# The fourth group's second layer by seven products in six of eight pairs

## The chip, the cores and the metric

The kernel runs on one core of one Trainium2 chip. The metric is the device time of one execution in microseconds (us), as the median of several runs. The engines are called by their names in the profile: PE (TensorE; PEld is its weight load), DVE (VectorE), ACT (ScalarE), POOL (GpSimd) and SP (SyncE, which issues most transfers).

## The reference

The input is 4 batches of 8 heads with 768 positions of 64 values. Each position attends to the first 8 positions and to the last 96 up to itself, with a bias that falls with the distance. The result, 3072 tokens of 512 values, goes through a two-layer network:

```python
h = x @ w_in                                                  # 512 -> 2048
g = np.where(h > 0.0, h, alpha * (np.exp(np.minimum(h, 0.0)) - 1.0))
return (g @ w_out).astype(np.float32)                         # 2048 -> 512
```

## The kernel before

**Groups and slices.** The tokens go in 12 groups of 256 (two tiles of 128). The 2048 hidden values go in 16 slices of 128. For a slice and a group, the first layer (`up`) makes a 128x256 block `h` in one PSUM bank, ACT and DVE make the activation `g` of it, and the second layer (`down`) adds the slice's product with its 128x512 weights to the output banks. Every factor is kept as a rounded part and a remainder (HI and LO; `gh` and `gl`), so that each product is three terms: `up` is 12 matmuls of 256 columns, and a plain `down` (line 880, in `moe`) is two tiles by three terms, 6 matmuls of 512 columns.

**Order of the groups.** The weights arrive in the first quarter. Groups one to three go through the slices together, four slices at a time, with partial outputs kept in the tiles `pa0` to `pa5`. Then the fourth group (index `NE` = 3; about 203 to 256 us) goes plainly through all 16 slices (`moe`), and groups five to twelve (index `SE` = 4 and on) go through `seven`. The attention of the next group runs beside: four visits per group, in which PE makes the scores of one pair of heads and the weighted values of an earlier one (lines 474 and 610), DVE, ACT and POOL make the softmax (lines 462, 464, 482, 580), and the probabilities are turned by a store to DRAM and a load back (lines 589 and 596).

**Seven products.** `seven` takes slices in pairs `j`. The activations of a pair are four blocks (two slices by two tiles), the weights four blocks (two slices by left and right half of 256 columns). The eight block products are replaced by seven: `combine` makes four sums of activation blocks on DVE (lines 733 to 736; tile `sum7`), rounds raw blocks and sums on ACT (`rh`, `sh`; line 303) and makes their remainders on DVE (`rl`, `sl`; line 311). `down` then multiplies them (line 768): products 1, 2, 4 first, then 6 and 5, then 3 and 7, each three matmuls of 256 columns, 21 in all. Products 2, 3 and 4 (as `mix` tiles) and 5 (in the right half of `w0`) need sums of weight blocks. The products stay apart in four banks `o0` to `o3` until the group's end, where one copy on ACT and seven adds on DVE (line 798) make the two output tiles.

**The weight sums.** `prepare`, one call per pair, adds up the whole weights (`hl`, line 672), makes four differences (`tf`), rounds each (`mix`, lines 303 and 305, ACT or POOL) and takes the remainder (line 311, DVE or POOL), and stores it to DRAM (line 668). This runs beside the end of group three and group four, in the order of `j`, in tiles `pa0` to `pa5`. `swap` then stores the old right half of each `w0` (line 695; needed for a rarely taken branch at the end) and loads the first sum in its place (line 696), after group four. Sums two to four are loaded again for each pair and group (line 751): three loads of 256 KB.

**Who sets the order.** The order of all work is written out ahead. Each piece of work (`p.add`) has a due time, engines it can run on with modelled costs, and the tiles it reads and writes; a list scheduler (`Plan.order`) takes on each engine what can start first and among these what is due first. `early` holds a piece back until a time. A tile class takes its places in the order of its pieces (`SLOTS`); each engine then runs its list strictly in that order, SP too, whose list holds all transfers and their waits. In groups one to four, `h` has four banks (`WIDE`: `h0`, `h1`, `v0`, `t0`); `seven` has two (`h0`, `h1`), since `v0` and `t0` are its banks `o2` and `o3`.

## Time and profile before

| | |
|---|---|
| median of 3 runs | 644.73 us (644.15 to 644.75) |
| the profiled execution | 644.23 us, of which the span of its instructions is 642.4 us |
| PE busy | 631.0 us, 98% of the span |
| PEld busy | 584.4 us, 91% |
| DVE busy | 492.7 us, 77% |
| ACT, POOL busy | 411.0 and 199.1 us |
| granted PE clock, mean | 0.997 |
| DMA | 149.82 MB, mean 233 GB/s |

Times in the trace run from the span's start. Matmuls are pipelined, so an engine that is 98% busy need not be at its peak; the distance from one start to the next says what an instruction takes of PE. An instruction that reads `x4` stands for four in a row. A landing time runs from the issue of a transfer to its semaphore.

### The profile page before, as it was taken

Reading aid. Unit: us, or ns where it says so; the run is one execution under the profiler, and the core shown is the slowest. Engines: PE = TensorE matmul, PEld = TensorE weight load, DVE = VectorE, ACT = ScalarE, POOL = GpSimd, SP = SyncE. Lnnn points to the kernel's source line nnn. Section 1 sums busy time; section 2 is a strip of 40 time slices with the busy share of each in tenths; the row PEclk is TensorE's granted clock in tenths of the full one; section 3 lists DMA queues with packets and bytes.
Section 4 is the critical chain, followed back from the end, with each engine's and each line's share of the span. In section 5 each row is a group of like instructions: output and inputs, shape, how many; then the busy total and the mean of one; then the engine's idle time right before and its main releaser. Section 6 shows DMA issues by size and latency. Waiting matters only on the chain.

```text
span 642.4 us, 19164 instructions
## 1 busy us (share of the span) xinstructions
PE 631.0 (98%) x7054; PEld 584.4 (91%) x7054; DVE 492.7 (77%) x1648; ACT 411.0 (64%) x1201; POOL 199.1 (31%) x500
## 2 busy tenths in 40 slices
PE   8999999999999999999999999999999999999996
PEld 5878888898888889999999999999999999999996
DVE  6999888899878975777777777777686777776654
ACT  6999776666644665666666566576566566654553
POOL 3557465465467672121121121112022022020000
PEclk9999999999999999999999999999999999999998
DMA  8979934231365899788888888888888788875542
GB/s 309 376 283 408 342 84 125 70 108 62 87 220 211 260 300 295 250 269 246 270 252 282 258 251 264 277 259 253 273 253 243 254 283 260 277 233 165 181 149 86
DMA packets 131171, 149.82 MB, mean 233 GB/s; under 512 B 63616, under 2 KB 82816, under 8 KB 131072
## 3 DMA queue, kind: packets, MB, share of 16 engines
q1 hardware_dynamic: 130784, 148.41, 71.7%
q8 instruction: 57, 0.93, 0.6%
q14 instruction: 42, 0.34, 0.2%
q10 hardware_dynamic: 288, 0.13, 0.1%
HBM read 117.57 MB, written 30.93 MB: 231 GB/s over the span
## 4 chain that ended last, share of the span: by engine, by line
PE 89%; DVE 4%; ACT 3%; DMA 2%; issue 1%; POOL 0%; DVEq 0%; POOLq 0%; ACTq 0%
PE h L712 28%; PE o L768 24%; PE o L880 13%; PE h L854 12%; PE s L610 5%; PE s L474 4%; PE pv L507 2%; DMA qk<-in_qkv_dram 1%; ACT pr L464 1%; PE t L527 1%; DMA n_raw<-in_n_dram 1%; DVE pr L462 1%; DMA mixed<-mix 1%; PE t L529 0%; DVE g L395 0%
## 5 line engine op out<-in xcount | busy, mean ns | idle before, releaser
L712 PE MATMUL h<-xh,w 128*128 128x256 f32 x1024 | 142.2, 280 | 0.8 <-DVE gg L722 0.8
L712 PEld LDWEIGHTS h<-xh,w 128*128 128x128 f32 x1024 | 129.8, 188 | 3.0 <-issue 1.2
L722 DVE SCALAR_TENSOR_TENSOR gg<-e,h 128x256 f32<-128x256 f32 x128 | 53.4, 417 | 76.0 <-ACT e L721 74.9
L580 POOL TENSOR_SCALAR pr<-pr,st 128x168 f32<-128x168 f32 x144 | 62.6, 435 | 152.1 <-DVE st L482 139.3
L464 ACT ACTIVATE pr<-pr,nmax 128x168 f32<-128x168 f32 x192 | 81.8, 427 | 16.9 <-DVE nmax L462 16.3
L720 ACT ACTIVATE e<-h 128x256 f32<-128x256 f32 x128 | 48.7, 381 | 58.4 <-PE h L712 58.4
L854 PEld LDWEIGHTS h<-xh,w 128*128 128x128 f32 x512 | 76.9, 188 | 9.9 <-DVE h L862 0.2
L880 PE MATMUL o<-w,gh 128*128 128x512 f32 x256 | 81.6, 400 | 0.4 <-DVE ob L912 0.4
L712 PE MATMUL h<-xl,w 128*128 128x256 f32 x512 | 81.8, 281 | 0.0
L854 PE MATMUL h<-xh,w 128*128 128x256 f32 x512 | 81.5, 282 | 0.0
L712 PEld LDWEIGHTS h<-xl,w 128*128 128x128 f32 x512 | 69.4, 188 | 2.0 <-issue 1.7
L462 DVE CUSTOM_DVE_ANT_0 pr<-s,far 128x168 f32<-128x168 f32 x192 | 53.3, 325 | 11.8 <-ACT xh L303 11.1
L311 POOL TENSOR_TENSOR w<-g,w 128x256 fp32r<-128x256 f32 x64 | 50.8, 816 | 35.7 <-ACT w L303 29.8
L303 ACT CAST sh<-sum 128x512 fp32r<-128x512 f32 x64 | 39.8, 621 | 30.9 <-DVE sum L736 30.9
L585 DVE STREAM_TRANSPOSE tr<-pr 128x192 f32<-128x192 f32 x144 | 50.0, 364 | 11.2 <-POOL pr L580 10.7
L721 ACT ACTIVATE e<-e 128x256 f32<-128x256 f32 x128 | 53.4, 417 | 3.6
L768 PE MATMUL o<-mix,sh 128*128 128x256 f32 x256 | 51.1, 281 | 0.0
L880 PEld LDWEIGHTS o<-w,gh 128*128 128x128 f32 x256 | 43.0, 188 | 7.9 <-ACT e L860 1.0
L451 POOL TENSOR_SCALAR qk<-qk,scale 128x256 f32<-128x256 f32 x14 | 8.0, 570 | 135.6 <-DMA qk<-in_qkv_dram 68.1
L311 DVE TENSOR_TENSOR sl<-sum,sh 128x512 fp32r<-128x512 f32 x64 | 44.2, 691 | 5.7 <-ACT sh L303 5.7
L768 PE MATMUL o<-w,sh 128*128 128x256 f32 x256 | 48.1, 280 | 0.0
L303 ACT CAST rh<-gg 128x384 fp32r<-128x384 f32 x64 | 32.8, 513 | 20.1 <-DVE gg L722 19.5
(142 smaller groups left out, 1418.9 us busy)
## 6 DMA issues: line engine op xcount, KB each, us to landing
mix<-mixed SPq DMA_DIRECT2D x192, 256.0 KB, 4.6
qk<-in_qkv_dram SPq DMA_DIRECT2D x48, 312.0 KB, 4.1
v<-in_qkv_dram SPq DMA_DIRECT2D x36, 384.0 KB, 5.0
dd<-tr SPq DMA_DIRECT2D x36, 384.0 KB, 4.6
pt<-dd SPq DMA_DIRECT2D x72, 192.0 KB, 3.8
bits<-in_w_in_dram SPq DMA_DIRECT2D x16, 512.0 KB, 8.5
bits<-in_w_out_dram SPq DMA_DIRECT2D x16, 512.0 KB, 9.7
mixed<-mix SPq DMA_DIRECT2D x32, 256.0 KB, 3.2
```

The source lines that it names most:

```text
L303: self.nc.scalar.copy(out, x)
L311: self.on(e).tensor_tensor(out, x, y, ALU.subtract)
L462: first = p.add((("DVE", 85 + 1.042 * LW, False),), lambda e: nc.vector.tensor_tensor_reduce(x(), s.t[:, i, :LW], tab, -(2.0 ** -(h + 1)), ...
L464: p.add(act(LW, extra=200), lambda e: nc.scalar.activation(x(), x(), AF.Exp, bias=nm, scale=-1.0, accum_out=st.t[:, n, 0:1]), [pr], [pr, s ...
L580: nc.gpsimd.tensor_scalar(pr.t[:, :LW], pr.t[:, :LW], st.t[:, n, 3:4], 1.0, ALU.mult, ALU.mult)
L585: nc.vector.transpose(tr.t[:, :, i, j], pr.t.rearrange("p (b r) -> p b r", r=32))
L712: nc.tensor.matmul(h.t, w1.t[:, s, cc * P:(cc + 1) * P], self.chunk(x, cc), start=n == 0 and s == HI and cc == 0, stop=n == 1 and cc == se ...
L721: p.add(act(W), lambda e: nc.scalar.activation(ex.t, ex.t, AF.Exp, scale=-1.0), [ex], [ex], d - 8000)
L722: p.add(dve(W), lambda e: nc.vector.scalar_tensor_tensor(gs(), ex.t, -1.0, h.t, ALU.add, ALU.max), [h, ex], [g], d - 8000)
L768: nc.tensor.matmul(acc[bank].t[:, half], a, b.t[:, LO if t == 1 else HI, x], start=j == 0 and t == 0 and n in first, stop=j == self.NFC // ...
L854: nc.tensor.matmul(h.t, w1.t[:, s, cc * P:(cc + 1) * P], self.chunk(x, cc), start=n == 0 and cc == 0, stop=n == 2 and cc == self.NCC - 1)
L880: nc.tensor.matmul(o.t[:, :at.stop - at.start], g.t[:, i * P:(i + 1) * P], w2.t[:, s, at], start=fc == f0 and n == 0 and s == HI, stop=fc ...
```

## The change

The fourth group goes through `seven` as well. Its first two pairs (`DIRECT` = 2) are multiplied plainly there, in `direct`: the eight block products, three terms each, as 24 matmuls of 256 columns, with the eighth output half in the free half of bank `o3`. Pairs three to eight go by seven products. `prepare` takes these six pairs first and the two plain ones last; the plain ones' pieces come after the fourth group's in the list. The first sum is written by ACT or POOL and DVE or POOL into the right half of `w0` itself, so its store and its reload are gone; the old half is stored before (`keep`), not earlier than a set time (138 us in the planner's clock for the first pair, 9 us more for each further one). Stored sums now use the class `mixed` with the two places `pa0` and `pa1`; the fourth group's loads use `pa2` to `pa5`, its `sum7` the places `io0` and `io1`. Its group end has one more add, for the eighth half. Its `h` has two banks, not four.

```diff
@@ -661,9 +661,11 @@
             return dve(n) + pool(n)
 
         def stored(n, tf, d):
-            x = self.sb("mix", "mix", [P, 2, M], F32R)
-            p.add(act(M) + pool(M, False), lambda e: self.copy(e, x.t[:, HI], tf.t), [tf], [x], d)
-            p.add(two(M), lambda e: self.minus(e, x.t[:, LO], tf.t, x.t[:, HI]), [tf, x], [x], d + 10)
+            x, at, after = (w0, right, [self.kept[j]]) if n == 1 else (self.sb("mixed", "mix", [P, 2, M], F32R), left, [])
+            p.add(act(M) + pool(M, False), lambda e: self.copy(e, x.t[:, HI, at], tf.t), [tf, *after], [x], d)
+            p.add(two(M), lambda e: self.minus(e, x.t[:, LO, at], tf.t, x.t[:, HI, at]), [tf, x], [x], d + 10)
+            if n == 1:
+                return
             s = self.mixed[j][n] = self.dr(f"mix{j}{n}", "mixed", [P, 2, M])
             p.add(sp(), lambda e: nc.sync.dma_start(s.t, x.t.bitcast(F32)), [x], [s], d + 30, nbytes=P * M * 8)
 
@@ -686,20 +688,18 @@
         stored(2, t2, due + 310)
         stored(4, less(r1, left, t2, slice(0, M), due + 400), due + 410)
 
-    def swap(self, j, due):
+    def keep(self, j, due):
 
         nc, p, M = self.nc, self.plan, self.DM // 2
-        w0, x = self.ws[1][2 * j], self.mixed[j][1]
-        right = slice(M, 2 * M)
+        w0 = self.ws[1][2 * j]
         self.kept[j] = kept = self.dr(f"kept{j}", "kept", [P, 2, M])
-        p.add(sp(), lambda e: nc.sync.dma_start(kept.t, w0.t[:, :, right].bitcast(F32)), [w0], [kept], due, nbytes=P * M * 8)
-        p.add(sp(), lambda e: nc.sync.dma_start(w0.t[:, :, right].bitcast(F32), x.t), [x, kept], [w0], due + 10, nbytes=P * M * 8)
-
-    def seven(self, rows, xh, xl, dues, step, last):
+        p.add(sp(), lambda e: nc.sync.dma_start(kept.t, w0.t[:, :, M:].bitcast(F32)), [w0], [kept], due, nbytes=P * M * 8, early=due)
+
+    def seven(self, rows, xh, xl, dues, step, last, plain=None):
 
         nc, p, M = self.nc, self.plan, self.DM // 2
         left, right = slice(0, M), slice(M, 2 * M)
-        acc = {}
+        acc, begun = {}, set()
         G = {}
 
         def up(fc, d):
@@ -723,7 +723,14 @@
 
         def combine(j, d):
             g = G[j]
-            s = self.sb("sum7", "sum7", [P, 4, P])
+            if j < (plain or 0):
+                gh, gl = (self.sb(x, x, [P, 4, P], F32R) for x in ("sh", "sl"))
+                whole = lambda x: x.t.rearrange("p a t -> p (a t)")
+                p.add(act(4 * P), lambda e: self.copy(e, whole(gh), whole(g)), [g], [gh], d - 8000)
+                p.add(dve(4 * P), lambda e: self.minus(e, whole(gl), whole(g), whole(gh)), [g, gh], [gl], d - 7000)
+                G[j] = gh, gl
+                return
+            s = self.sb("sum7", "sum7", [P, 4, P], slots=self.SUMS if plain is not None else None)
             rh, rl = self.sb("rh", "rh", [P, 3, P], F32R), self.sb("rl", "rl", [P, 3, P], F32R)
             sh, sl = (self.sb(x, x, [P, 4, P], F32R) for x in ("sh", "sl"))
             flat = lambda x: x.rearrange("p a t -> p (a t)")
@@ -742,36 +749,66 @@
             p.add(dve(4 * P), lambda e: self.minus(e, flat(sl.t), flat(s.t), flat(sh.t)), [s, sh], [sl], d - 6500)
             G[j] = rh, rl, sh, sl
 
+        def opened():
+            if not acc:
+                for i in range(6 if last else 4):
+                    acc[i] = self.bank(f"o{i}", "o", [P, 2, M])
+
+        def direct(j, d):
+
+            gh, gl = G.pop(j)
+            ws = self.ws[1][2 * j:2 * j + 2]
+            opened()
+            for f, w in enumerate(ws):
+                for c, terms in enumerate(((0, 1), (2,))):
+                    todo = []
+                    for i in range(NT):
+                        for half, x in enumerate((left, right)):
+                            bank, at = self.OF[last][self.PLAIN[i][half]]
+                            for t in terms:
+                                todo.append((bank, at, i, x, t, bank not in begun))
+                                begun.add(bank)
+
+                    def mm2(e, todo=todo, f=f, w=w):
+                        for bank, at, i, x, t, start in todo:
+                            nc.tensor.matmul(acc[bank].t[:, at], (gh, gl)[t == 2].t[:, 2 * f + i], w.t[:, LO if t == 1 else HI, x], start=start, stop=False)
+
+                    p.add(pe(4 * len(terms) * M), mm2, [(gh, gl)[c], w], list(dict.fromkeys(acc[b] for b, *_ in todo)), d + 2 * f + c)
+
         def down(j, d):
+            if j < (plain or 0):
+                return direct(j, d)
             w0, w1 = self.ws[1][2 * j], self.ws[1][2 * j + 1]
             rh, rl, sh, sl = G.pop(j)
             mix = {}
             for n in (4, 3, 2):
-                x = mix[n] = self.sb("mix", "mix", [P, 2, M], F32R)
+                x = mix[n] = self.sb("mix", "mix", [P, 2, M], F32R, slots=self.SLOTS["mix"][2:] if plain is not None else None)
                 p.add(sp(), lambda e, x=x, n=n: nc.sync.dma_start(x.t.bitcast(F32), self.mixed[j][n].t), [self.mixed[j][n]], [x], d - 6000 - 10 * n, nbytes=P * M * 8)
-            if not acc:
-                for i in range(6 if last else 4):
-                    acc[i] = self.bank(f"o{i}", "o", [P, 2, M])
+            opened()
             end = last and j == self.NFC // 2 - 1
             of = self.OF[last]
             raw = {1: 0, 4: 1, 2: 2}
             mixed = {5: 0, 6: 1, 7: 2, 3: 3}
             right_of = {1: (w0, left), 2: (w1, left), 3: (w1, right), 5: (w0, right), 4: (mix[4], left), 6: (mix[2], left), 7: (mix[3], left)}
-            first = (1, 6, 7, 2, 5, 3) if last else (1, 6, 3, 4)
-
-            def mm2(e, ns, terms):
+
+            def mm2(e, ns, terms, starts):
                 for n in ns:
                     bank, half = of[n]
                     b, x = right_of[n]
                     for t in terms:
                         a = ((rh, rl)[t == 2].t[:, raw[n]] if n in raw else (sh, sl)[t == 2].t[:, mixed[n]])
                         nc.tensor.matmul(acc[bank].t[:, half], a, b.t[:, LO if t == 1 else HI, x],
-                                         start=j == 0 and t == 0 and n in first, stop=j == self.NFC // 2 - 1 and t == 2 and n in ((6, 7, 4, 2, 5, 3) if last else (2, 5, 7, 4)))
+                                         start=t == 0 and n in starts, stop=j == self.NFC // 2 - 1 and t == 2 and n in ((6, 7, 4, 2, 5, 3) if last else (2, 5, 7, 4)))
 
             def put(ns, terms, x):
                 g = [x for n in ns for x, ts in zip((rh, rl) if n in raw else (sh, sl), ((0, 1), (2,))) if set(ts) & set(terms)]
                 ws = [right_of[n][0] for n in ns]
-                p.add(pe(len(ns) * len(terms) * M), lambda e: mm2(e, ns, terms), list(dict.fromkeys(g + ws)), list(dict.fromkeys(acc[of[n][0]] for n in ns)), x)
+                starts = []
+                for n in ns:
+                    if of[n][0] not in begun:
+                        begun.add(of[n][0])
+                        starts.append(n)
+                p.add(pe(len(ns) * len(terms) * M), lambda e: mm2(e, ns, terms, starts), list(dict.fromkeys(g + ws)), list(dict.fromkeys(acc[of[n][0]] for n in ns)), x)
 
             if end:
                 put([1, 4, 2], (0, 1), d)
@@ -832,6 +869,8 @@
         add(lo, 0, o(lo, 1), q(4), [lo, P_(4)])
         add(hi, 0, o(hi, 0), q(2), [hi, P_(2)])
         add(lo, 1, o(lo, 1), q(5), [lo, P_(5)])
+        if plain:
+            add(lo, 1, o(lo, 1), q(8), [lo, P_(8)])
         store(0, None)
         add(hi, 1, o(hi, 1), q(5), [hi, P_(5)])
         add(hi, 1, o(hi, 1), q(3), [hi, P_(3)])
@@ -979,17 +1018,17 @@
                 b, gi = groups[n]
                 if f0 == 0 and f1 < NFC:
                     parts[n] = [self.sb("part", "part", [P, self.DM]) for _ in range(NT)]
-                if n >= self.SE:
-                    self.seven(b * self.S + gi * W, *X[n], d, self.STEP, n == len(groups) - 1)
+                if n >= self.NE:
+                    self.seven(b * self.S + gi * W, *X[n], d, self.STEP, n == len(groups) - 1, self.DIRECT if n == self.NE else None)
                     return
                 self.moe(b * self.S + gi * W, *X[n], f0, f1, d, self.STEP, parts.get(n), n < self.NE, n == len(groups) - 1)
             todo.append((d[f0], moe))
         self.kept, self.mixed = {}, {}
-        for j in range(NFC // 2):
-            d = [x for (n, _, _), x in zip(segs, dues) if n == self.SE - 1][-1][2 * j + 1] + 2 * self.STEP
-            e = self.PREPARE[0] + j * self.PREPARE[1]
-            todo.append((start[self.NE] - 1.0, lambda j=j, e=e: self.prepare(j, e + self.PREPARE[2], e)))
-            todo.append((start[self.SE] - 1.0, lambda j=j, d=d: self.swap(j, d)))
+        pairs = [*range(self.DIRECT, NFC // 2), *range(self.DIRECT)]
+        for k, j in enumerate(pairs):
+            e = self.PREPARE[0] + k * self.PREPARE[1]
+            todo.append((start[self.NE] - 2.0, lambda j=j, e=e: self.keep(j, e - self.KEEP)))
+            todo.append((start[self.NE + (j < self.DIRECT)] - 1.0, lambda j=j, e=e: self.prepare(j, e + self.PREPARE[2], e)))
         for _, f in sorted(todo, key=lambda x: x[0]):
             f()
 
@@ -997,8 +1036,10 @@
     T0, STEP0, STEP, LEAD, NE = 34000.0, 3000.0, 3000.0, (4000.0, 12000.0), 3
 
     LATE, FIRST_LOADS = 12, 22
-    PREPARE, SE = (168000.0, 9000.0, 6000.0), 4
...
+    PREPARE, DIRECT = (168000.0, 9000.0, 6000.0), 2
+    PLAIN = (4, 8), (2, 3)
+    SUMS, KEEP = ["io0", "io1"], 30000.0
...
```

## Rows read from the trace of the kernel before

**Rows 1.** Busy time of each engine in three stretches (first line: columns).

```profile
core 0: us, PE busy (x) PEld busy (x) DVE busy (x) ACT busy (x) POOL busy (x), PEclk, DMA share, GB/s
80.00:203.00 123.00, 122.82 (x1022) 108.63 (x1020) 105.40 (x276) 78.44 (x222) 71.77 (x128) 1.00 0.37 115
206.00:256.00 50.00, 50.00 (x538) 44.09 (x537) 37.88 (x124) 30.08 (x96) 28.02 (x62) 1.00 0.91 290
256.00:306.00 50.00, 50.00 (x627) 48.51 (x627) 37.08 (x137) 32.27 (x95) 8.35 (x33) 1.00 0.81 249
```

**Rows 2.** What PE waited for after 80 us: total us, times, longest.

```profile
PE h L712 <- DVE gg L722: 0.8, 1, 0.8
PE o L880 <- DVE ob L912: 0.4, 1, 0.4
```

**Rows 3.** PE in order of time, fourth group: start us, us, instruction.

```profile
219.70 0.63 PE L854 MATMUL h<-xl,w 128*128 128x256 f32 x4
220.17 0.63 PE L880 MATMUL o<-w,gl 128*128 128x512 f32 x2
220.64 0.63 PE L880 MATMUL o<-w,gh 128*128 128x512 f32 x2
```

**Rows 4.** The page, costliest groups: busy us, mean ns of one.

```profile
L712 PEld LDWEIGHTS h<-xh,w 128*128 128x128 f32 x1024 | 129.8, 188 | 3.0 <-issue 1.2
```

**Rows 5.** PE in order of time, products of the fifth group and after.

```profile
256.31 0.63 PE L768 MATMUL o<-w,rh 128*128 128x256 f32 x4
299.93 0.63 PE L768 MATMUL o<-w,rh 128*128 128x256 f32 x4
305.19 0.63 PE L768 MATMUL o<-w,rh 128*128 128x256 f32 x4
312.14 0.63 PE L768 MATMUL o<-w,rh 128*128 128x256 f32 x4
313.20 0.40 PE L768 MATMUL o<-mix,sh 128*128 128x256 f32 x2
```

**Rows 6.** DVE in order of time, handover from fifth to sixth group.

```profile
301.45 0.29 DVE L733 TENSOR_TENSOR sum<-gg 128x128 f32<-128x128 f32 x1
302.39 0.41 DVE L798 TENSOR_TENSOR ob<-ob,o 128x256 f32<-128x256 f32 x1
302.72 0.55 DVE L311 TENSOR_TENSOR rl<-gg,rh 128x384 fp32r<-128x384 f32 x1
303.52 0.68 DVE L311 TENSOR_TENSOR sl<-sum,sh 128x512 fp32r<-128x512 f32 x1
304.12 1.41 DVE L798 TENSOR_TENSOR ob<-ob,o 128x256 f32<-128x256 f32 x4
305.77 0.42 DVE L798 TENSOR_TENSOR ob<-ob,o 128x256 f32<-128x256 f32 x1
```

**Rows 7.** SP in order of time, the second load of a pair.

```profile
313.81 0.38 SPq L751 DMA_DIRECT2D mix<-mixed  x1
```

**Rows 8.** Line 751, six loads of prepared slices, 206 to 256: us to landing.

```profile
DMA to landing us min/median/max: 4.5/4.9/5.6
```

**Rows 9.** PE in order of time, attention visits in the fourth group.

```profile
227.32 0.93 PE L610 MATMUL s<-pt,v 64*64 64x64 f32 x48
236.93 0.93 PE L610 MATMUL s<-pt,v 64*64 64x64 f32 x48
```

**Rows 10.** Lines 668 (stores of sums), 695 (kept halves), each with its landing times.

```profile
L668 SPq DMA_DIRECT2D mixed<-mix x32: 319/326/747, 182.0 to 245.5; - x32
DMA to landing us min/median/max: 2.0/3.2/5.6
L695 SPq DMA_DIRECT2D kept<-w x8: 525/552/629, 55.2 to 169.7; - x8
DMA to landing us min/median/max: 2.4/3.5/9.1
```

**Rows 11.** SP's own waits, 306 to 356: total us, times, longest.

```profile
SPq L596 <- DMA dd<-tr: 10.8, 4, 3.9
```

6 lines of the change are left out of this document (3 added, 3 removed).

## The prediction

> **What bounds the kernel now.** I first read busy time by engine in stretches [rows 1]. TensorE (PE) is busy 122.8 of 123 us from 80 to 203, then 50.00 of 50 in the two stretches after 206; VectorE (DVE) has room and the granted clock is 1.00. So from 80 us to almost the end the time is the sum of PE's columns: an edit pays what it takes off PE, less the waits it makes. The list of what PE waited for names only two waits after 80 us [rows 2]: 0.8 us for the first layer's activation (line 722) and 0.4 us for a bank to be emptied (line 912).
>
> The order of PE's work gives the price of a column [rows 3]. From one start to the next, four matmuls of 256 columns take 0.47 us and two of 512 take 0.47 us: 0.1175 us per 256 columns, either way.
>
> **The change, part by part.** The profiled execution took 644.23 us (span 642.4); the median of the runs is 0.5 us above it, so the sum is made on the first and moved up by 0.5.
>
> *Products.* A pair now costs 12 matmuls of 512 columns, or 24 units of 0.1175 us. By seven products it costs 21 units. Six pairs save 6 x 3 x 0.1175 = **2.1 us**, all on PE. The two plain pairs become 24 matmuls of 256 columns: the same columns, so nothing, with twice the weight loads. Those loads hide today wherever products are 256 wide: PE stays at 50.00 while its weight loads fill 48.5 [rows 1]. What hides them is the matmul in front; uncovered, one costs at most its recorded 188 ns [rows 4].
>
> Against this stands a rule of the Trainium skill, "TensorE: Matmul & The Clock Gate", section "Back-to-back issue gap": in a stream of weight load and matmul, 128 columns take about 81 ns and 512 about 131 ns. Between these, 256 columns would take about 98 ns (my estimate), and the sum would read 2 x 0.78 + 6 x 0.49 = 4.5 us slower. The trace disagrees: 235 ns for 512 and 117.5 for 256 [rows 3].
>
> *The bank wait.* The 0.4 us at line 912 is the fourth group's first second-layer matmul waiting for the third group's banks. By seven products second-layer work begins only after two pairs' first layers, so that wait should go: **-0.4 us**, or 0 if another wait takes its place.
>
> *The handover of banks.* The fourth group's output now lies in four banks that eight adds must empty before the fifth group fills them. Such a handover stands at 302 to 306 [rows 5, 6]: adds start at 302.39, four run back to back from 304.12 (one add takes its engine 0.33 us, 302.39 to 302.72) and the seventh at 305.77. The next group's first product at 305.19 needs the fourth add, done near 304.9, a margin of 0.3. Now its bank also holds the eighth half, added sixth: done near 305.5, so PE waits about **+0.3 us** (0 if PE's order is shifted, 1.0 if three adds fall behind preparation work).
>
> *Loads of prepared slices.* 18 loads are new (6 pairs x 3) and the fourth group may hold four slices at a time, not six. A pair's first load finds the spare slot; the third waits for the second-used slot of the pair before. In the trace that load goes out at 313.81 [rows 7], 1.67 us after its pair's products began at 312.14, and would be needed 1.06 us into the next pair's products (312.14 to 313.20). Where no attention work stands between, pairs are 305.19 - 299.93 = 5.26 us apart [rows 5], so 5.26 + 1.06 - 1.67 = 4.65 us are left. Loads in this stretch landed in 4.5 to 5.6 us, median 4.9 [rows 8]: late by 0.25. With attention work between, pairs are 6.95 us apart (305.19 to 312.14) and nothing is late. Of five handovers between pairs by seven, at most two hold attention (visits at 227.32 and 236.93 [rows 9]); three are bare: 3 x 0.25 = **+0.7 us**. Ends: 0 at 4.5 us, 3 x 0.95 = 2.9 at 5.6. I take the median, the row of this very stretch.
>
> *Transfers in all.* Gone are eight stores of first sums and the eight reloads of line 696 that put them in place in the fifth group's time; eight stores of the kept halves move from 55 to 170 us to later, still mostly before 206 [rows 10]. Sixteen less and eighteen more of 256 KB: nothing, although DMA is busy 0.91 in this stretch [rows 1]. On SP's queue, 18 issues replace 16. A kept half is stored some 30 us ahead of the write that waits for it; stores took at most 9.1 us [rows 10], so the cast and the subtraction that now write into the weight tile find it free, and neither ScalarE, VectorE, GpSimd nor what is queued behind them waits. For the two plain pairs this write also waits for the fourth group's products with the old half; these are its first two pairs, while their sums are now prepared seventh and eighth, after 229 (182.0 + 6 x 7.9, [rows 10]).
>
> *VectorE.* A pair by seven takes four sums 0.94 (301.45 to 302.39), two subtractions 0.47 (0.80 from 302.72 to 303.52, less one add) and 0.60 (303.52 to 304.12) [rows 6], against two of about 0.33 now: +1.35, times six +8.1 us. The stretch 206 to 256 goes from 37.9 to 46 busy of 50. I cost it at nothing: the order of work is a list sorted by due times, in which preparation of the last pairs stands behind the group's own work, and those sums are needed late (below). The eight adds at the end (2.6 us, where ScalarE made two copies) are counted in the handover. The cover is thinner, though: the fourth group's first layer falls from four PSUM banks to two. The end on the other side is four waits like the 0.8 of [rows 2], 3.2 us.
>
> *Space.* The sums of the fourth group use the output tiles of the first three groups; the first is written only with the third pair, some 12 us after those groups' work has ended. Nothing.
>
> *Readiness.* 32 sums are stored from 182.0 to 245.5 [rows 10], 7.9 us per pair, so six pairs are ready by 230, while the last pair by seven is multiplied near 250. The two plain pairs come last, and the second is wanted near 263 (one pair after 256.31 [rows 5]). But stores now have two buffers: 24 stores, two at a time, at about 1.1 us of work and 3.2 us of landing (the median of [rows 10]) end at 182 + 12 x 4.3 = 234; at 5.6 us landing, at 262, a little late. I take 0.
>
> **Sum:** -2.1 - 0.4 + 0.3 + 0.7 = -1.5. Profiled 642.7, median **643.2 us**.
>
> **The rivals.** A measurement of this kernel can tell about 0.2%, 1.3 us, from no change: "same" is 643.4 to 646.0.
>
> *Eaten up (same).* Loads land at 5.6 (+2.9) or activations come late (up to 3.2), and one such loss takes the saving: -2.5 + 0.3 + 2.9 = +0.7, about 645.4; at half the loss 644.0. For it: VectorE at 92%, two first-layer banks, DMA at 0.91. Against it: from 80 to 203 VectorE was 86% busy (105.4 of 123) and PE lost 0.2 us. Chance 0.41, with in it 0.02 that the change doesn't do what it says because the sums are not ready.
>
> *Slower: SP's queue.* SP issues in order. The store of turned probabilities must land before SP may issue the load behind it; in one stretch SP stood there four times for 10.8 us, up to 3.9 [rows 11]. With six slots that is free. With four, a slice's load queued behind such a wait is late by all of it. It decides once the added waits pass 2.2 + 1.3 = 3.5 us; two of the mean 2.7 on bare handovers give 5.4, so -2.5 + 0.3 + 5.4 = +3.2, about 647.9. Against it: the bare handovers are those with least attention traffic. Chance 0.10.
>
> *Paced by weight loads (slower).* If 256-column matmuls went at their 188 ns weight loads [rows 4], a plain pair would cost 24 x 0.188 = 4.51 us against 2.82 and a pair by seven 3.95: 2 x 1.69 + 6 x 1.13 = +10.2, 654.9. The spacing in [rows 3] speaks plainly against it. Chance 0.01. The Trainium skill's rule above points the same way, less far.
>
> *The forecast (faster),* most of the 2.1 kept: 642.0 to 643.4. Chance 0.48.
>
> **How the numbers follow.** Without late loads and with the bank wait gone the time is 644.7 - 2.5 + 0.3 = 642.5, or 642.2 with no handover cost either; a little for orders of work that shift earlier on gives 642.0. Upwards the range takes in the eaten-up case to 645.6. Outside lie the slower cases (0.11) and a few hundredths at both edges. The forecast's own range is 642.0 to 643.4. Faster 0.48, same 0.41, slower 0.11.
>
> **What would show it.** In the changed trace: 18 units of 256 columns less on PE in the fourth group; no wait on line 912; a wait of PE for slices of some 0.2 us in each bare handover, none with attention between; VectorE near 46 of 50 from 206 to 256, PE still at 50. The fifth group's first product should come about 1.5 us before 256.31. The forecast is wrong if PE shows waits for activations (line 722) in the fourth group, if slices land behind a long wait of SP, or if PE's starts in a plain pair lie further apart than 0.1175 us.

## The result, and the profile after

The changed kernel takes **653.06 us** (median of 5 runs, 651.93 to 655.42), the kernel before 644.4 (5 runs beside it): ratio 1.0146, 95% interval 1.0119 to 1.0172. It is 1.5% slower, where 0.2% faster was forecast; the time lies above the range.

The profiled execution took 653.97 us (span 652.2). Busy time by engine in the three stretches of [rows 1], in the same columns, with the changed kernel:

```profile
80.00:203.00 123.00, 123.00 (x1024) 108.90 (x1023) 105.96 (x274) 80.69 (x224) 63.84 (x119) 1.00 0.38 111
206.00:256.00 50.00, 41.53 (x520) 38.71 (x519) 41.88 (x126) 24.95 (x81) 33.11 (x61) 0.93 0.78 248
256.00:306.00 50.00, 50.00 (x630) 48.51 (x629) 38.64 (x141) 32.81 (x98) 9.95 (x36) 1.00 0.95 280
```

The loss is in the fourth group's stretch: TensorE stands still for 8.47 of the 50 us from 206 to 256, and the granted clock averages 0.93. In the stretches beside it TensorE stays full. What it waited for from 80 to 640 (total us, times, longest, as in [rows 2]; the waits for `pt<-dd` lie between 456 and 556, all others in the fourth group):

```profile
PE o L800 <- DMA mix<-mixed: 3.0, 3, 1.3
PE h L712 <- DVE gg L722: 2.5, 2, 1.7
PE s L610 <- issue: 2.2, 1, 2.2
PE s L610 <- DMA pt<-dd: 1.0, 2, 0.7
PE o L800 <- DVE rl L311: 0.7, 1, 0.7
```

The wait at line 912 (now 951) is gone, as forecast. In its place stand landings of loaded slices (line 800), the activation of the first layer (line 712), the attention visit's bank (line 610) and the remainders of the activations (`rl`). TensorE in order of time, those of its starts that waited (in brackets: idle us, releaser), and the fifth group's first product:

```profile
216.15 1.21 PE L712 MATMUL h<-xh,w 128*128 128x256 f32 x8 [1.73 <-DVE gg L722]
...
228.69 0.50 PE L800 MATMUL o<-w,rl 128*128 128x256 f32 x2 [0.69 <-DVE rl L311]
229.96 0.47 PE L800 MATMUL o<-mix,sh 128*128 128x256 f32 x2 [0.65 <-DMA mix<-mixed]
238.43 0.48 PE L800 MATMUL o<-mix,sh 128*128 128x256 f32 x2 [1.30 <-DMA mix<-mixed]
246.49 0.86 PE L610 MATMUL s<-pt,v 64*64 64x64 f32 x43 [2.24 <-issue]
249.38 0.77 PE L800 MATMUL o<-mix,sh 128*128 128x256 f32 x2 [1.04 <-DMA mix<-mixed]
...
268.04 0.74 PE L800 MATMUL o<-w,rh 128*128 128x256 f32 x4
```

The largest, 2.24 us, is labelled "issue". What was late is read from GpSimd and VectorE just before it (each in order of time):

```profile
244.28 0.40 POOL L305 CAST mix<-tf 128x256 fp32r<-128x256 f32 x1 [3.30 <-DMA mixed<-mix]
244.65 1.26 POOL L674 TENSOR_TENSOR hl<-w 128x512 f32<-128x512 f32 x1
```

VectorE of the same kernel, same view:

```profile
244.72 1.47 DVE L311 TENSOR_TENSOR mix<-tf,mix 128x256 fp32r<-128x256 f32 x1 [1.46 <-POOL mix L305]
246.11 0.28 DVE L311 TENSOR_TENSOR xl<-s,xh 128x128 fp32r<-128x128 f32 x1
```

GpSimd stood 3.30 us until a store of an earlier sum had landed and freed one of the **two store places**; VectorE stood behind that cast; its subtraction then took 1.47 us beside GpSimd's addition; and only after it came the subtraction at 246.11 that empties the visit's bank. The wait of 1.73 at 216.15 has the same head: a GpSimd cast (212.82) that stood 4.33 us for a store, VectorE (213.26) 2.38 behind it, and the activation behind that. From 200 to 262 GpSimd stood so six times, 12.2 us in all.

The `rl` wait at 228.69 shows a **second cause**, VectorE's sums of activations beside GpSimd (VectorE, then GpSimd, each in order of time):

```profile
225.69 0.64 DVE L740 TENSOR_TENSOR sum<-gg 128x128 f32<-128x128 f32 x1
226.26 0.83 DVE L741 TENSOR_TENSOR sum<-gg 128x128 f32<-128x128 f32 x1
227.01 0.83 DVE L742 TENSOR_TENSOR sum<-sum,gg 128x128 f32<-128x128 f32 x1
227.87 0.29 DVE L743 TENSOR_TENSOR sum<-gg,sum 128x128 f32<-128x128 f32 x1
```

GpSimd of the same kernel:

```profile
225.46 0.73 POOL L311 TENSOR_TENSOR tf<-hl,hl 128x256 f32<-128x256 f32 x1
226.15 0.79 POOL L311 TENSOR_TENSOR w<-tf,w 128x256 fp32r<-128x256 f32 x1
226.90 0.79 POOL L311 TENSOR_TENSOR mix<-tf,mix 128x256 fp32r<-128x256 f32 x1
```

Each of the first three sums ends just after the GpSimd instruction beside it; the fourth, with GpSimd free, takes 0.29, as in [rows 6].

The **third** is the loads. From 214 to 262, sixteen of them (one line of the changed kernel's line 786) landed as follows, where [rows 8] had 4.5/4.9/5.6:

```profile
DMA to landing us min/median/max: 2.6/5.3/6.7
```

They were also issued late. The loads behind the three waits are the third ones of their pairs; SyncE issued them at 224.3, 233.1 and 242.9, and they landed 5.2 to 6.3 us later. In SyncE's order they stood behind stores of sums and behind transfers of the attention (SyncE of the same kernel, in order of time; `x2` is two issues):

```profile
229.88 2.61 SPq L670 DMA_DIRECT2D mixed<-mix  x2
232.54 0.93 SPq L786 DMA_DIRECT2D mix<-mixed  x2
...
239.33 1.28 SPq L596 DMA_DIRECT2D pt<-dd  x2
240.70 0.59 SPq L670 DMA_DIRECT2D mixed<-mix  x1
...
242.93 0.85 SPq L786 DMA_DIRECT2D mix<-mixed  x2
```

The **fourth** is the clock. Windows of 1 us of the changed kernel, columns as above:

```profile
246.00:247.00 1.00, 0.51 (x33) 0.54 (x37) 0.96 (x6) 0.51 (x1) 0.00 (x0) 1.00 0.96 329
247.00:248.00 1.00, 1.00 (x44) 0.80 (x33) 1.00 (x4) 0.05 (x1) 0.82 (x3) 0.75 1.00 368
248.00:249.00 1.00, 0.34 (x6) 0.00 (x0) 0.99 (x4) 1.00 (x4) 1.00 (x3) 0.50 1.06 408
...
253.00:254.00 1.00, 1.00 (x7) 1.00 (x6) 0.25 (x2) 0.00 (x0) 0.94 (x2) 0.50 0.62 160
254.00:255.00 1.00, 1.00 (x9) 1.00 (x9) 0.86 (x1) 0.30 (x2) 1.00 (x3) 0.84 0.93 348
```

TensorE stood 2.24 us, ran the visit's small matmuls from 246.49, and in these the grant fell (0.75 in 247 to 248). It stays 0.50 (1.2 of 2.4 GHz) till about 254; the wait of 1.04 us lies inside that stretch. A 256-column matmul then takes 0.213 us (250.16 to 250.80 for three) against 0.1175, so the 4.7 us from 249.38 cost some 2.1 us, with the visit before them 2 to 2.5 (an estimate).

**The account** between the two profiled executions (9.7 us): 8.5 of waits in 206 to 256, 2 to 2.5 of clock, 0.5 more idle time before 80 and nothing net elsewhere, less 2.1 of columns: 8.9 to 9.4.

### The profile page after: what moved, and what is told of

Same layout as the page of the kernel before. It is cut to its first block, busy times and chain, and to the rows that moved or that the text cites. A ratio compares the mean times of both kernels' runs of the same rounds, so it can differ in the third digit from the quotient of the medians.

```text
span 652.2 us, 19325 instructions
## 1 busy us (share of the span) xinstructions
PE 631.1 (97%) x7132; PEld 588.4 (90%) x7132; DVE 506.6 (78%) x1674; ACT 413.7 (63%) x1204; POOL 200.3 (31%) x498
## 4 chain that ended last, share of the span: by engine, by line
PE 76%; DMA 9%; DVE 6%; POOL 3%; ACT 3%; issue 2%; SPq 1%; POOLq 0%; DVEq 0%; ACTq 0%
PE h L712 26%; PE o L800 23%; PE h L893 8%; PE o L919 8%; PE s L610 4%; PE s L474 3%; DMA mixed<-mix 2%; DMA pt<-dd 2%; DMA mix<-mixed 2%; PE pv L507 2%; DMA dd<-tr 1%; POOL pr L580 1%; ACT pr L464 1%; DMA v<-in_qkv_dram 1%; PE t L527 1%
## 5 line engine op out<-in xcount | busy, mean ns | idle before, releaser
L722 DVE SCALAR_TENSOR_TENSOR gg<-e,h 128x256 f32<-128x256 f32 x144 | 59.7, 415 | 75.9 <-ACT e L721 74.6
L720 ACT ACTIVATE e<-h 128x256 f32<-128x256 f32 x144 | 54.5, 379 | 60.2 <-PE h L712 59.7
L712 PE MATMUL h<-xl,w 128*128 128x256 f32 x576 | 91.8, 281 | 0.0
L712 PEld LDWEIGHTS h<-xl,w 128*128 128x128 f32 x576 | 78.2, 189 | 2.0 <-issue 1.7
L721 ACT ACTIVATE e<-e 128x256 f32<-128x256 f32 x144 | 59.9, 416 | 3.8
L919 PE MATMUL o<-w,gh 128*128 128x512 f32 x192 | 61.2, 399 | 0.0
L800 PE MATMUL o<-mix,sh 128*128 128x256 f32 x280 | 56.9, 284 | 3.0 <-DMA mix<-mixed 3.0
L311 DVE TENSOR_TENSOR sl<-sum,sh 128x512 fp32r<-128x512 f32 x70 | 49.2, 703 | 5.0 <-ACT sh L303 5.0
L800 PEld LDWEIGHTS o<-mix,sh 128*128 128x128 f32 x280 | 43.2, 190 | 4.1 <-ACT e L721 2.3
L800 PE MATMUL o<-w,rh 128*128 128x256 f32 x280 | 45.6, 285 | 0.0
```

Of the source, the lines that this page charges most:

```text
L311: self.on(e).tensor_tensor(out, x, y, ALU.subtract)
L712: nc.tensor.matmul(h.t, w1.t[:, s, cc * P:(cc + 1) * P], self.chunk(x, cc), start=n == 0 and s == HI and cc == 0, stop=n == 1 and cc == se ...
L720: p.add(act(W, True), lambda e: nc.scalar.activation(ex.t, h.t, AF.Relu, scale=-1.0), [h], [ex], d - 8000)
L721: p.add(act(W), lambda e: nc.scalar.activation(ex.t, ex.t, AF.Exp, scale=-1.0), [ex], [ex], d - 8000)
L722: p.add(dve(W), lambda e: nc.vector.scalar_tensor_tensor(gs(), ex.t, -1.0, h.t, ALU.add, ALU.max), [h, ex], [g], d - 8000)
L800: nc.tensor.matmul(acc[bank].t[:, half], a, b.t[:, LO if t == 1 else HI, x], start=t == 0 and n in starts, stop=j == self.NFC // 2 - 1 and ...
```

## The experiments

All times are medians of several runs beside the kernel before on the same chip (643.1 to 644.5). The theories: **S**, two store places hold up GpSimd, and VectorE and all its work behind it; **L**, four places for loads make them late; **T**, the list of work assumes transfers that land too early; **V**, VectorE (or the bank cut) is late by itself. P is S and L together, Q is SyncE's queue. A loss in us below is against the kernel before beside it.

| Run | us | ratio | 95% interval |
|---|---|---|---|
| e1 share six | 651.60 | 1.0102 | 1.0077–1.0127 |
| e2 before, two store places | 650.92 | 1.0097 | 1.0078–1.0115 |
| e3 before, four load places | 674.75 | 1.0481 | 1.0455–1.0508 |
| e4 all plain | 648.41 | 1.0060 | 1.0036–1.0084 |
| e5 list told | 654.13 | 1.0167 | 1.0149–1.0186 |
| e6 four store places | 649.76 | 1.0109 | 1.0062–1.0156 |
| e8 eight places, told | 651.31 | 1.0109 | 1.0080–1.0138 |
| e10 before, two h banks | 644.48 | 1.0012 | 0.9993–1.0031 |
| e11 six load places | 650.87 | 1.0099 | 1.0070–1.0129 |
| e12 four pairs plain | 647.61 | 1.0061 | 1.0039–1.0083 |
| e13 one sum per pair | 648.85 | 1.0076 | 1.0048–1.0104 |
| e14 sums 18 us earlier | 654.85 | 1.0166 | 1.0138–1.0194 |
| e15 no loads, six places | 647.76 | 1.0066 | 1.0049–1.0083 |
| e15b no loads, two places | 646.47 | 1.0053 | 1.0032–1.0074 |
| e16 e12, loads by ScalarE | 647.95 | 1.0072 | 1.0048–1.0096 |
| e17 e6, loads by ScalarE | 650.04 | 1.0100 | 1.0072–1.0128 |
| e18 e15, GpSimd only fills | 643.12 | 0.9982 | 0.9967–0.9998 |
| e19 e12, casts by ScalarE | 646.58 | 1.0037 | 1.0022–1.0051 |

### Each suspect alone, in the kernel before

**Two store places** (the fifth group's first three pairs load into the other four, so that the two classes don't meet):

```diff
-            x = self.sb("mix", "mix", [P, 2, M], F32R)
+            x = self.sb("mixed", "mix", [P, 2, M], F32R)
...
+             "mixed": ["pa0", "pa1"],
```

> The kernel before, with one thing of the change: stored sums have only the places pa0 and pa1 (and the first three pairs of the fifth group load into pa2 to pa5). The fourth group stays plain, with four first-layer banks. Theory S: GpSimd waits for stores to land here too, and PE loses 2 to 5 us in 206-256: 647-650. Theories L and V: no loss, 644-645.

It loses 6.4 us, with the plain fourth group of before. GpSimd stands for landing stores (its waits from 160 to 262 in this run; before had 1.0 us in two):

```profile
POOL mix L305 <- DMA mixed<-mix: 25.3, 18, 2.7
```

and TensorE is busy only 45.34 of the 50 us from 206 (columns of [rows 1]):

```profile
206.00:256.00 50.00, 45.34 (x490) 38.49 (x490) 36.01 (x116) 25.16 (x88) 29.51 (x65) 0.98 0.82 248
```

TensorE's longest wait there, 1.8 us, is for a remainder that VectorE makes (`gl`). S is shown for the kernel before: this edit alone, which the prediction costed at nothing, is dearer there than all that the products save.

**Four load places** for all eight groups by seven:

```diff
-                x = mix[n] = self.sb("mix", "mix", [P, 2, M], F32R)
+                x = mix[n] = self.sb("mix", "mix", [P, 2, M], F32R, slots=self.SLOTS["mix"][2:])
```

> The kernel before, with one thing of the change: all eight groups by seven load their prepared slices into four places instead of six; stores of sums are as before. Theory L: each group loses 1 to 3 us on bare handovers, 652-668 in all; by the term of the prediction (0.7 us a group) 650. Theory S: loads are late only where stores crowd the transfers, so 644-646.

It loses 30.2 us over eight groups, 3.8 for a group. TensorE's waits from 256 to 606 in this run:

```profile
PE o L768 <- DMA mix<-mixed: 13.7, 15, 1.7
PE o L768 <- DVE rl L311: 3.7, 2, 1.9
PE o L768 <- ACT sh L303: 2.0, 1, 2.0
```

TensorE stands still for 19.8 of the 350 us from 256 to 606 (0.8 in the kernel before), of which 13.7 for landings, and the granted clock in its three stretches of 50 us from 306 on is 0.97. L is shown for the groups by seven. The rest of the loss isn't parted further.

**Two first-layer banks** in the fourth group:

```diff
-            h = self.bank("h", "h", [P, W], self.WIDE if wide else None)
+            h = self.bank("h", "h", [P, W], self.WIDE if wide and rows < self.NE * W else None)
```

> The kernel before with one thing of the change: the fourth group's first layer has two PSUM banks instead of four. Theory V (two banks and a full VectorE make the activations late): PE waits at the first layer for 1 to 3 us, 645.5-648. Theories S and L: no loss, 644-645.

No loss that can be told from nothing: the "thinner cover" of the prediction costs nothing by itself. Beside a VectorE as busy as the change makes it, it was not tried.

### Parts of the change undone

**All pairs plainly** (the constant DIRECT from 2 to 8, the output copied straight from its banks, the fifth group's first loads in the four places the stores leave):

```diff
-    PREPARE, DIRECT = (168000.0, 9000.0, 6000.0), 2
+    PREPARE, DIRECT = (168000.0, 9000.0, 6000.0), 8
```

> The changed kernel with all eight pairs of the fourth group multiplied plainly: no product saved there, no load of prepared slices in it; two first-layer banks, two places for stored sums, first sum in its place as in the change. It loses the 2.1 us of columns against the change. Theory S: the waits for stores stay, 648-651. Theory L: without loads there is nothing to wait for, 644-645. Theory V: VectorE is relieved of the sums (8 us), 644-646.

Without any product by seven or load in the fourth group, 3.9 us are lost still; two store places remain, with 24 stores where e2 had 32, and GpSimd waits 10.9 us for them (160 to 262). But `direct` also takes the remainder of an activation from two tiles in SBUF (`sl<-gg,sh`: 0.65 to 1.22 us for the same 512 columns), where the plain group before reads one of them from PSUM. So e4 does not part S from the VectorE cause found below.

**The list told of late landings** (2.4 us more on the stores and on the fourth group's loads):

```diff
-                end = max(end, bw + 1500.0)
+                end = max(end, bw + 1500.0) + op.lag
```

> The changed kernel, places unchanged, but the list that orders the work counts 2.4 us more for the landing of each stored sum and of each prepared slice of the fourth group (it counts 2.2 to 2.4 us now; the trace shows 3.0 for stores and 4.6 for loads). Theory P (places alone): what a place can turn over per us is fixed by the landing, so the time stays at 650-653. Theory T (the list's belief: its order puts GpSimd's cast and PE's products where the place or slice is not there yet, though other work could stand in front): waits of GpSimd for stores and of PE for slices go down to under 1.5 us together, 645-648.

GpSimd's waits for stores (160 to 262) fall from 17.4 to 7.2 us, but TensorE's for landings stay at 3.1, those for the activation rise to 5.5, and the time does not fall. T brings no time.

### Other shares of the same places

Stores and loads share six (e1); stores get pa0, pa1, xl0a, xl0b, the differences two instead of four (e6); all eight are shared and the list is told (e8); loads get all six, stores xl0a and xl0b (e11). The line of places, for e6:

```diff
-             "mixed": ["pa0", "pa1"],
+             "mixed": ["pa0", "pa1", "xl0a", "xl0b"],
...
-             "tf": ["tf0", "tf1", "xl0a", "xl0b"],
+             "tf": ["tf0", "tf1"],
```

> Stored sums and the fourth group's loads of prepared slices share all six places pa0 to pa5 instead of two and four. Theory S (two places for stored sums hold GpSimd until a store has landed, VectorE stands behind it, PE behind that: 1.73 + 2.24 us of PE's waits, and most of the 3.5 us at half clock): the time falls from 653 to 645-647, and GpSimd's wait of 12.2 us for stores goes. Theory L (four places for loads: 3.0 us of waits for slices): the places are as many in all, so it stays at 650-653. Theory V (VectorE is simply too full, 0.81 + 0.69 us and the rest from its queue): 652-653.

> The changed kernel with four places for stored sums: two of the four buffers of the weight differences (xl0a, xl0b) are given to them, the differences keep two; loads keep four places. Theory S: without the waits behind stores (4.0 us of PE's 8.5, and the half-clock stretch that followed the longest) 646-648.5, with GpSimd's wait for stores under 4 us. Theory L: the loads' part stays, and alone holds the time at 649-652.

> The changed kernel with both cures: stored sums and the fourth group's loads share eight places (pa0 to pa5, xl0a, xl0b; the weight differences keep two), and the list counts 2.4 us more for their landing. Theories S and L: most of the 8.5 us of PE's waits and the clock loss go, 643-646, at or under the kernel before. Theory V: VectorE stays too full beside the seven products, 647-650.

> The changed kernel with all six part places for the loads of the fourth group's pairs and two other places (those of the old differences) for the stored sums, so that stores and loads share nothing. Theory L (four load places are the main loss): PE's waits on landed mixes vanish and the time falls from 653 to about 648. Theory S (two store places are the main loss): GpSimd's waits for stored sums stay at 10 us or more, PE keeps waiting for VectorE and the time stays at 651 to 654. Both as measured alone (6.4 us for two store places, 3.8 us per group for four load places): 649 to 651.

All end between 649.8 and 651.6, a loss of 6.2 to 7.8 against 8.7. In e11 TensorE no longer waits for a landing, as L expects, but waits for VectorE take their place (`gg` 3.1 us, `sl` 1.1), and GpSimd still stands 9.8 us for stores. In e6 no wait of GpSimd for a store is left (160 to 262), TensorE's waits for landings are down to 0.6 us with the same four load places, and 6.2 us are lost. Places explain a part at most: each of the four intervals still overlaps the changed kernel's (1.0119 to 1.0172), and no share gives the rest back.

**Four pairs plainly**, with e6's places (DIRECT = 4), and **preparation 18 us earlier**, with e6's places (168000.0 to 150000.0):

> The changed kernel with four store places and four pairs plainly instead of two. The columns saved fall from 2.1 to 1.4 us. Theory P (the loss comes from sums being prepared, stored and loaded back in the same stretch as the pairs by seven, so fewer such pairs that start later meet less of it): 645 to 647.5, with PE's waits in the fourth group below 2 us. Theory V (the loss goes with the VectorE work of each pair by seven): about two thirds of the loss of four places with two pairs plainly (649.8), so 648. If neither bears on it, 650 to 651.

> The changed kernel with four store places and the preparation of the sums begun 18 us earlier (due at 150 instead of 168 us). Theory P (stores and loads meet in the fourth group): most pairs are stored before the group begins, and the time falls to 644 to 647. Theory V: VectorE's work in 206 to 256 falls from 45.5 to about 40 us and the time falls as far; the two part only if PE still waits for landings (P) or for VectorE (V). If the loss is in the pairs themselves (clock, loads, the list), 649 to 651.

e12 loses 3.4 us: fewer pairs by seven lose less. Its 647.6 lies between P's 647.5 and V's 648 and parts neither; its 3.3 us of TensorE's waits in the group are all for landings, where P gave under 2. e14 loses 10.6, against both: VectorE's work is moved into 181 to 206, where TensorE is now full to only 22.63 of 25 at clock 0.93.

**Another queue.** e16 is e12, e17 is e6, with the loads issued by ScalarE:

```diff
-                p.add(sp(), lambda e, x=x, n=n: nc.sync.dma_start(x.t.bitcast(F32), self.mixed[j][n].t), [self.mixed[j][n]], [x], d - 6000 - 10 * n, nbytes=P * M * 8)
+                on, q = ((("ACT", 60.0, False),), nc.scalar) if plain is not None else (sp(), nc.sync)
+                p.add(on, lambda e, x=x, n=n, q=q: q.dma_start(x.t.bitcast(F32), self.mixed[j][n].t), [self.mixed[j][n]], [x], d - 6000 - 10 * n, nbytes=P * M * 8)
```

> Four store places, four pairs plainly, and the fourth group's loads issued from ScalarE's queue instead of SyncE's. Theory Q (the loads are late since they stand in SyncE's queue behind stores whose sums GpSimd and VectorE have not finished): PE's 3.3 us of waits on landings shrink to under 1 and the time falls from 647.6 to 644 to 646. Theory P (they wait for places or for the transfer itself): no change, 647 to 648.5. ScalarE now waits for places too; if that is dear, above 648.5.

> Four store places, two pairs plainly, the fourth group's loads on ScalarE's queue. Theory Q: from 649.8 to 645 to 647. Theory P: 649 to 651. Above 651 if ScalarE's own waits for places delay the activations.

Neither gains time. In e16 the waits for landings go as Q expects, from 3.3 us in e12 to 0.5, but 1.6 us for ScalarE and 0.7 for turned probabilities take their place; in e17 the landings stay (1.7 us, 0.6 in e6). Q's queue is part of why loads are late, and this cure is no gain.

### VectorE

**One sum per pair** in the fourth group, e6's places and order of work:

```diff
+                if plain is not None:
+                    V.tensor_tensor(flat(s.t), flat(g.t), flat(g.t), ALU.add)
+                    return
```

> The changed kernel with four store places, in the same order of work, where the four sums of activations of each of the fourth group's pairs are one addition of 512 columns in place of four of 128 that wait for each other; the sums are thereby left out. VectorE is rid of some 1 us per pair, 6 us in all. Theory V (VectorE, slowed beside GpSimd, is late for the group's pairs): PE's waits for VectorE and ScalarE in the fourth group shrink to under 1 us and the time falls by 2 to 4 us from 649.8, to 646 to 648. Theory P (places and landings): no change, 649 to 651.

4.6 us lost against e6's 6.2; the intervals overlap. By itself it looks small, so the next runs took the loads away instead:

```diff
-            for n in (4, 3, 2):
+            for n in (4, 3, 2) if plain is None else ():
...
-            right_of = {1: (w0, left), 2: (w1, left), 3: (w1, right), 5: (w0, right), 4: (mix[4], left), 6: (mix[2], left), 7: (mix[3], left)}
+            right_of = {1: (w0, left), 2: (w1, left), 3: (w1, right), 5: (w0, right)}
+            right_of |= {n: (mix[m], left) if mix else (w1, left) for n, m in ((4, 4), (6, 2), (7, 3))}
```

> The changed kernel with the fourth group's loads of prepared slices left out: its products of the second, third and fourth sums read resident slices instead, and all six part places go to the stored sums. Left out: the right values of three products in each of six pairs. What is left of the change is its columns, its activation sums and the work of VectorE and ScalarE on them. If the whole loss lies in places, landings and the queues that carry them: 642 to 644.5, the forecast's sum. If a part lies in VectorE, ScalarE or the order of the list: 645 to 648, with PE's waits on them.

> The same without the fourth group's loads, but with the two store places of the changed kernel. Two store places cost 6.4 us with the plain fourth group; if that holds here too, 648 to 651, with GpSimd's waits for stored sums at 10 us or more. If the loads were what made two places dear (their transfers slow the stores), 643 to 646.

These two were the surprise. With no load and six store places 4.7 us are lost still, so places and landings are not all. And without the loads two store places cost nothing more (3.4 us lost, intervals overlapping), though GpSimd still waits 11.8 us for them (25.3 in e2). Why the same two places cost 6.4 us in e2, whose fourth group has no loads of slices either, but 32 stores for 24, is not shown. Stores of 256 KB land in 2.5 to 2.7 us in these two runs (medians, 206 to 256), against 3.6 in e2 and 3.5 in the changed kernel.

What remains in e15 is VectorE, busy 46.59 of the 50 us from 206 (columns of [rows 1]):

```profile
206.00:256.00 50.00, 46.38 (x586) 44.04 (x585) 46.59 (x134) 28.57 (x92) 37.08 (x68) 1.00 0.66 206
```

TensorE's waits from 181 to 306 in this run:

```profile
PE s L610 <- issue: 2.0, 1, 2.0
PE o L801 <- DVE rl L311: 1.0, 1, 1.0
PE o L801 <- DVE sl L311: 0.6, 2, 0.4
```

Its four sums on VectorE, 206 to 256 (busy us, mean ns, idle before):

```profile
L741 DVE TENSOR_TENSOR sum<-gg 128x128 f32<-128x128 f32 x6 | 4.7, 780 | 0.0
L740 DVE TENSOR_TENSOR sum<-gg 128x128 f32<-128x128 f32 x6 | 2.9, 475 | 0.0
L743 DVE TENSOR_TENSOR sum<-gg,sum 128x128 f32<-128x128 f32 x6 | 2.3, 376 | 0.2
L742 DVE TENSOR_TENSOR sum<-sum,gg 128x128 f32<-128x128 f32 x6 | 1.9, 315 | 0.0
```

VectorE is busy without a pause before the visit that waits 2.03 us (from 232.66 to past 242, one short gap of 0.22), and one sum in there took 1.38 us beside a GpSimd addition of 1.34. So the order of work was kept and GpSimd's reads for the sums were taken out:

```diff
+        def fill(e, x):
+            if e == "POOL":
+                nc.gpsimd.memset(x, 0.01)
+            return e == "POOL"
...
-            p.add(two(M), lambda e: self.minus(e, tf.t, a.t[:, ax], b.t[:, bx]), [a, b], [tf], d)
+            p.add(two(M), lambda e: fill(e, tf.t) or self.minus(e, tf.t, a.t[:, ax], b.t[:, bx]), [a, b], [tf], d)
```

> The run without the fourth group's loads and with six store places (4.6 us of idle TensorE between 181 and 306, 647.8), where every step of the sums' preparation that falls to GpSimd writes a constant in place of its cast, sum or difference; the order of work and VectorE's own instructions stay. Left out besides: the values of those sums. Theory G (GpSimd's reads of SBUF hold up VectorE's additions and differences of two SBUF operands, which the activation sums of the pairs by seven are and the plain path's, read from PSUM, are not): the fourth group's 128-column sums fall from 315 to 780 ns towards 280 to 300, VectorE's busy time in 206 to 256 from 46.6 to about 42, the idle time of TensorE to under 1.5 us, and the time to 642.5 to 645. Theory N (it is the number of VectorE's instructions alone): the busy time stays above 45 and the time at 646.5 to 648.

643.12, the loss gone: 0.65 us under the kernel before, 0.1 to 2.1 by the interval. The same stretch of this run:

```profile
206.00:256.00 50.00, 49.99 (x676) 47.77 (x676) 41.41 (x149) 31.87 (x98) 18.15 (x60) 1.00 0.69 212
```

and its four sums:

```profile
L746 DVE TENSOR_TENSOR sum<-gg 128x128 f32<-128x128 f32 x7 | 2.1, 302 | 0.0
L748 DVE TENSOR_TENSOR sum<-gg,sum 128x128 f32<-128x128 f32 x7 | 2.0, 292 | 0.2
L747 DVE TENSOR_TENSOR sum<-sum,gg 128x128 f32<-128x128 f32 x7 | 2.0, 285 | 0.0
L745 DVE TENSOR_TENSOR sum<-gg 128x128 f32<-128x128 f32 x7 | 2.0, 281 | 0.1
```

VectorE does more (149 instructions against 134) in 5.2 us less, TensorE is full from 80 to 606 but for 0.01, and no wait of it is listed there. GpSimd still waits 9.2 us for stores there (160 to 262), at no cost. The run comes out as theory G expects, and N fails. It doesn't part GpSimd's reads from its being sooner done (37.08 to 18.15 us of work). The durations speak for the reads: from 181 to 306 VectorE is busy 105.93 us for 313 instructions in e15, and 97.99 us for 332 in e18.

**Casts by ScalarE alone**, nothing left out:

```diff
-            p.add(act(M) + pool(M, False), lambda e: self.copy(e, x.t[:, HI, at], tf.t), [tf, *after], [x], d)
+            p.add(act(M), lambda e: self.copy(e, x.t[:, HI, at], tf.t), [tf, *after], [x], d)
```

> Four store places, four pairs plainly, and the casts of the prepared sums on ScalarE alone, where GpSimd did about two thirds of them. Nothing is left out. Theory G: GpSimd has some 6 us less work beside VectorE in 206 to 256, VectorE's sums shorten, SyncE's queue waits less for GpSimd's part of the stored sums, and the time falls from 647.6 to 645.5 to 647. If ScalarE becomes late instead: 648 to 650. No version of it is expected below the kernel before by more than 0.2%.

646.58, 1.0037: the best whole version of the change, still behind the kernel before. It loses 2.8 us against e12's 3.4, with overlapping intervals, so the casts' part isn't clear of noise. Landings remain (2.7 us of TensorE's waits). No version that beats the kernel before was found.

## Why the prediction was wrong, point by point

*Products: right in price.* In the changed kernel a pair by seven takes 2.50 us, from its first product to what follows it:

```profile
255.91 0.63 PE L800 MATMUL o<-w,rh 128*128 128x256 f32 x4
258.41 1.10 PE L712 MATMUL h<-xh,w 128*128 128x256 f32 x8
```

That is 0.32 us less than a plain pair by [rows 3]; six make 1.9 of the forecast's 2.1. The plain pairs run at 0.115 us per 256 columns (24 matmuls in 2.76 us, 204.28 to 207.04), so the pacing by weight loads did not come; that its 654.9 lies near the time measured is chance. In e18 the fifth group's first product starts at 255.47, behind a visit of 1.43 us that comes later in the kernel before: without it 2.3 us ahead of the 256.31 there. The profiled span of e18 is 3.7 us shorter than before, but that execution is the fastest of its eleven. The medians differ by 0.65 us, and where the other executions of e18 lose is not traced.

*The bank wait and the handover:* the first went; the handover's 0.3 did not show (TensorE 50.00 of 50 from 256 to 306).

*"Readiness. But stores now have two buffers … I take 0":* **the first step that failed.** It asked when the last sum is stored: by 234, at worst 262. The last store went out at 261.3, and no product waited for it. It did not ask what the prediction itself names elsewhere: who stands behind the instruction that waits. A cast for a new sum stands in GpSimd's order with the next work, its subtraction in VectorE's, and the first layer's activations and the visits' banks behind those. In the kernel before it costs 6.4 us alone (e2); in the changed kernel it heads the waits of 1.73 and 2.24. How much of the 8.7 it makes there is less sure: four places bring back 2.4 us, with overlapping intervals (e6), and without the loads two cost no more than six (e15b).

*"Loads of prepared slices … +0.7":* **mis-sized.** 3.0 us of waits in the changed kernel, 3.8 for a group alone (e3), beyond the term's end of 2.9. Three waits came, as many as counted, but that is luck: they average 1.0 us in place of 0.25, and two of them have a visit between, where the prediction has nothing late. What failed is the time of issue. The term sends a pair's third load 1.67 us after the products of the pair before begin; here it went 3.6, 5.9 and 8.7 us after them (they begin at 220.7, 227.1 and 234.3), behind other work of SyncE. The landings add less: 5.2 to 6.3 us, where the term took 4.9.

*"VectorE … I cost it at nothing":* **the third failure, by size the first, and the one that stays when the others are gone** (e15 to e18: 4.7 us lost to 0.7 gained). Its 0.94 us for four sums comes from [rows 6], in a stretch where GpSimd works little (8.35 of 50 us [rows 1]). In the fourth group GpSimd prepares sums, and the same addition takes up to 0.83 (1.38 in e15). The plain path's subtraction reads its first operand from PSUM and does not suffer; in the kernel before, 200 to 256 (min/median/max ns):

```profile
L311 DVE TENSOR_TENSOR gl<-h,gh x16: 385/424/426, 200.7 to 247.9; 128x256 fp32r<-128x256 f32 x16
```

The same duration holds where GpSimd subtracts beside it (205.67: 0.42) and where it does nothing (200.68: 0.42). The end of 3.2 us named for this term was nearer than the 0 chosen: e15, where little but this is left, loses 4.7. The Trainium skill, "SBUF — State Buffer", section "Who interferes with whom", has this rule: a VectorE instruction with two SBUF inputs contends with a GpSimd instruction that reads SBUF, not with one that only writes, and one with at most one SBUF input, outside its two-port modes, does not. The traces agree on all three: 0.83 us beside GpSimd's subtractions, 0.28 to 0.30 in the mean beside its fills (e18), and 0.43 at most where one operand lies in PSUM.

*The clock* was not in the sum: behind a wait of 2.24 us and a visit's small matmuls it stood at 0.50 till about 254, which cost 2 to 2.5 us.

*The rivals.* "Eaten up" named late loads and late activations, but let one of them take the saving; both came, and store places with them. "Slower: SP's queue" foresaw the sign and part of the way: the load of 242.9 stood behind the load of turned probabilities at 239.33, for which SyncE had waited 3.4 us. But giving the loads another queue gained no time (e16, e17).

The losses of single runs don't add up: 6.4 and 3.8 alone make more than the 8.7 lost, and taking out one lets the next appear. Taken away one after the other they run from 8.7 to 6.2 (e6: no wait for a store), to 4.7 (e15: no loads) and to a gain of 0.7 (e18: GpSimd only fills). The first two steps lie within overlapping intervals; the last, 5.3 us, is clear. How the 8.7 would be shared in another order stays open. What is shown is that GpSimd's work on the sums beside VectorE is enough to undo the saving (e15 against e18), that two store places (e2) and four load places (e3) are so in the kernel before, and that the loss is gone when the loads and GpSimd's reads are both gone.

## What to carry to other kernels

When a buffer class shrinks, don't ask only whether its last user is in time: look up which engine's order the first waiting instruction stands in, and what stands behind it there. Take a load's time of issue from its queue's order in the stretch that is meant, with the other transfers that stand there. Take an instruction's duration from a stretch with the same neighbours; an addition of two SBUF operands on VectorE has two prices, with GpSimd idle and with GpSimd reading, and here work moved from PSUM operands to SBUF operands paid the second. In this kernel, whose TensorE was full, 2 us of columns saved in the stretch where the other engines are busiest cost more than they gave.

## What the runs showed of the hardware that was not expected

- VectorE's 128x128 addition takes 0.28 us where GpSimd does little (median of line 741 from 262 to 640), and up to 1.38 beside a GpSimd addition of 1.34, ending 0.15 us after it (239.28, 239.13; e15); beside GpSimd fills it stays at 0.28 to 0.30 in the mean (e18).
- TensorE's grant fell to 0.50 in a visit's small matmuls behind a wait of 2.24 us, stayed there through a wait of 1.04, and rose again near 254.
- A 256 KB store landed in 2.5 us (median) with DMA 0.66 busy (e15) and in 4.6 with it 0.91 busy (before), both from 206 to 256. The share alone does not tell the time: in e18, with 0.69, it was 3.4.
